# A gated attention and ReGLU backward pass: one matrix product and some transposes moved to other places

## The chip, the cores and the metric

The kernel runs on one core of a Trainium2 chip. The metric is device time in microseconds (us), the time of one execution on the chip. Times come from repeated runs; the profile comes from one execution of its own, whose time stands beside its span below.

## The reference

The reference computes a forward pass and its gradients with respect to seven inputs. Shapes: S = 2048 tokens, D = 512, F = 1376, 32 heads of 16, all bfloat16.

```python
qkv = (x @ wqkv).reshape(B, S, 3, H, Dh)...          # A: attention, window of 256 keys
p = softmax(where(mask, q k^T * Dh**-0.5, -1e9))
a = (p v) @ wo
gate = x @ W_gate; gate = gate * (gate > 0)          # B: ReGLU
h = gate * (x @ W_up)
b = h @ W_down
g = sigmoid((x * gate_w).sum(-1))
out = g * a + (1 - g) * b
# returned: out and the gradients of x, wqkv, wo, W_gate, W_up, W_down, gate_w for grad_out
```

## The kernel before, in words

There are three stages, and TensorE (PE) has one queue of instructions through all of them, in the order in which the program writes them. Most of it is written under a manual schedule, so the order on each engine is that of the Python code.

**FFN stage (0 to 251 us).** 44 steps: 11 chunks of F (128 columns each) by 4 groups of 512 tokens. A step computes gate, up and dh (`gate`, `up`, `dh`, L365 to L387), and some steps later the weight gradients of its chunk (`weights`, L402). The product h of a step is a tile hT with F on partitions and 512 tokens along the row. `turn_h` transposes it by DMA for the gradient of W_down, and `keep` (L398, called at L474) stores it to the DRAM tensor hT_d from ScalarE's DMA queue, as it does dgT and duT. The gradient of W_down of the last chunk is copied to the constant tile gw_b (L425), which later holds gate_w for the last stage. The activations db_r and db_T have tiles of their own in this stage.

**Attention stage (251 to 719 us).** Four head groups c of eight heads. In the profiled execution their first score matmuls start at 251.2, 354.1, 469.7 and 585.1 us. A group has 16 query tiles j of 128 tokens, and a query tile has up to six units: key block j ("d", diagonal), j - 1 ("m", middle) and j - 2 ("f", far), each in two halves of four heads. That makes 90 units a group, 360 in all. A unit is

- a score matmul ST of 512 columns (`front`, L681), its exponential on ScalarE (L691) and, for d and f, a mask on GpSimd (L693, L696), which gives Pu;
- a matmul dPT of 512 columns (`front_dp`, L705) one unit later, and the product Pd = Pu * dPT on VectorE (L710) two units later;
- 16 narrow matmuls of row sums (`rowsum`, L719 and L721) four units later, the value LAG;
- the transposes of Pu and Pd by 128 x 128 blocks (`flip`, L730). Where `u.dma` is set (L669), they are made by a DMA transpose on SP's queue, three units behind the front. Otherwise TensorE makes eight transposes (L748) into a PSUM tile pt, which ScalarE or VectorE copies out. Before, d units and m units of the first three groups go by DMA in pairs of halves (128 x 2048 elements), and all f units go by TensorE;
- later, 16 narrow matmuls CD per transposed unit (`cd_piece`, L532), which read the transposed tiles. The pieces wait in a list with the unit from which each may be issued: for the youngest query tile five units behind its last row sum.

PSUM tiles of tag TR (two banks) serve pt, the projections pp and the gradients wps in turn.

Between the units the planner (the `while` loop from L894) puts fillers: the six parts of the next projection (`project_parts`, L123: Q, dO, their DMA transpose, K, V, and the transposes of K and V), and pieces of the weight gradient of the group before (`grad_parts`, L623). A credit decides when: each unit adds SLOT - 0.63 us (L942), minus 0.44 if the unit that is LAG behind is transposed by TensorE; each filler takes its cost; a due time forces a projection that would come too late. Projected K and V lie in three buffers in rotation (one in pool pjA, two in pool pj). The table `plan` (L616) says behind which projection the weights of the last stage are loaded; those of W_down (`loads`, L599) and wo come last, in the fourth group.

**Last stage (719 to 910 us).** Eight groups of two query tiles. `load_group` (L817) loads, one group ahead, h (hT_g), dgT, duT, grad_out rows (go), attention outputs (o_g) and, by one DMA transpose from dqkvo_d, the tile T. hT, T and go of a group share one slot of pool st (tag rows_st, two buffers, also used by the rows of the head groups), the slots of the others come from pool g6. Per tile of 128 tokens TensorE runs dwo (4 matmuls of 512 columns, L1014), bps = h x W_down (11, L1033), aps (4, L1037), dxps from dgT and duT (22, L1060), four narrow dgw and dxps from T (12, L1064). This stage is ordered by the framework, not by hand.

Of the kernel before, what the change touches and what calls it, by code (L numbers as in the profile page):

```python
# [22 lines left out]
def kernel(  # L23
# [20 lines left out]
    nc = tc.nc  # L44
# [37 lines left out]
    hT_d = dram.tile([F, S], BF, name="hT_d")  # L82
# [29 lines left out]
    if True:  # L112
# [84 lines left out]

    with ExitStack() as p1, tc.manual_schedule():
# [3 lines left out]
        db_r = ap1.tile([P, NT, D], BF, name="db_r")  # L202
        db_T = ap1.tile([P, DC, S], BF, name="db_T")
# [198 lines left out]
        def weights(k):  # L402
# [25 lines left out]
            evac(dst[:], acc["d"][:], "act")  # L428

            def store():  # L430
# [4 lines left out]
                nc.sync.dma_start(out_6[k.fsl, :], dst[:])  # L435
# [6 lines left out]

        DA0 = 2 * NTG
# [4 lines left out]
        for n in range(N1 + 8):  # L448
# [24 lines left out]
            if at(3):  # L473
                keep(at(3), (hT_d, at(3).hT[:]))  # L474
# [30 lines left out]
            if n in (N1 + 2, N1 + 3, N1 + 4):  # L505
                second.pop(0)()
            z = n - DA0 - NT - 2
# [6 lines left out]
    if True:  # L514
        st = p3.enter_context(tc.tile_pool(name="attst", bufs=2))
# [70 lines left out]
        def load_rows(name, src, k, dst):  # L586
            W6[(name, k)] = dst
            skip = max(0, (k + 1) * P - src.shape[0])
            if skip:
                nc.gpsimd.memset(dst[0:skip, :], 0.0)  # L590
            nc.sync.dma_start(dst[skip:P, :], src[k * P:(k + 1) * P - skip, :])

# [6 lines left out]
        def loads(name, src, k0, tag):  # L599
            def one(k):  # L600
                if (tag, "t") not in W6:
                    W6[(tag, "t")] = slot(tag)
                load_rows(name, src, k, W6[(tag, "t")][:, k - k0, :])
            return [lambda k=k: one(k) for k in range(k0, min(k0 + 4, FC))]

        def load_wo():
            t = pjA.tile([P, 2, TGW], BF, tag="zT", name="wo_z")
            for k in range(2):
                load_rows("wo", A_wo, k, t[:, k, :])
            for k in range(2, DC):  # L610
                load_rows("wo", A_wo, k, pjA.tile([P, TGW], BF, tag="T", bufs=2, name="wo_t")[:])

        def load_gw():
            nc.sync.dma_start(gw_b[:], gate_w.partition_broadcast(P))

        plan = {2: [load_gw], 5: turns("wqkv", A_wqkv, 0, 4, "p0"), 7: turns("wqkv", A_wqkv, 4, 8, "p1"),  # L616
# [4 lines left out]
                15: loads("Wd", B_W_down, 0, "x3") + [lambda: clear("Wu")] + loads("Wd", B_W_down, 4, "d3") + loads("Wd", B_W_down, 8, "p3") + [load_wo]}  # L621
# [31 lines left out]

        class Unit:
# [3 lines left out]
        for c in range(DC):  # L658
            for j in range(NT):
                order = [(k, h) for k, h in ((j - 1, 0), (j - 1, 1), (j - 2, 0), (j, 0), (j, 1), (j - 2, 1)) if k >= 0]  # L660
                for kb, half in order:
# [7 lines left out]
                    u.dma = u.pair or (u.role == "m" and half == 0 and (c < DC - 1 or j < 10))  # L669
# [5 lines left out]
        def front(u):  # L675
# [6 lines left out]
            if not u.own:  # L682
                if u.half == 0:
                    kind = "m" if u.c == DC - 1 and u.j == 12 else u.role
                    tag = f"PP{kind}"
                    pairs[(u.c, u.j, u.kb)] = wk.tile([P, 2, 2, HH, P], BF, tag=tag, bufs=3, name=tag)
# [20 lines left out]
        def gradp(u):  # L707
            if u.own:
                u.Pd = wk.tile([P, HH, P], BF, tag="Pd", bufs=2, name="Pd")
# [102 lines left out]
        def early_f(i):  # L812
            flat = wq.tile([P, 2, TPG, NP, P], BF, tag=f"z{i}", name=f"f{i}")[:].rearrange("p w k h q -> p (w k h q)")
            S2[f"f{i}"] = flat[:, 0:FC * GT * P].rearrange("p (c s) -> p c s", c=FC)
            load_f(S2[f"f{i}"], (hT_d, dgT_d)[i], slice(0, GT * P))

        def load_group(g):  # L817
            gsl = slice(g * GT * P, (g + 1) * GT * P)
            if g == 0:
# [315 lines left out]
```

## Time and profile before

| What | Value |
|---|---|
| Time, median of 3 runs | 911.95 us (910.37 to 912.51) |
| Time of the profiled execution | 911.74 us |
| Its span, first to last instruction | 910.0 us |
| TensorE (PE) busy, instructions | 897.0 us (99%), 10711 |
| Weight loads (PEld) busy | 568.2 us (62%) |
| VectorE (DVE) busy | 510.3 us (56%) |
| ScalarE (ACT) busy | 443.2 us (49%) |
| GpSimd (POOL) busy | 494.2 us (54%) |
| Granted TensorE clock, whole span | 1.000 |
| DMA, whole span | 169.06 MB, mean 186 GB/s |

PE is TensorE's matmuls, PEld its weight loads, SP the engine whose queue issues most DMAs, ACTq and POOLq the DMA queues of ScalarE and GpSimd. L681 is line 681 of the kernel. A matmul is recorded from its issue to its modelled end, so that neighbours overlap. The DMA share is the mean busy share of 16 DMA engines; it can exceed 1, since several packets of one engine can be under way. The chain of waits follows the work that ended last back to what released it.

### The profile page before, as it was taken

To read this page: it belongs to the slowest core of one execution; us is meant where nothing else is said; L and a number is where in the kernel's file an instruction comes from. 1 tells how busy PE (TensorE), PEld (TensorE's weight loads), DVE (VectorE), ACT (ScalarE), POOL (GpSimd) and SP (SyncE) were. 2 spreads that over 40 slices of the span, in tenths; PEclk is the share of its full clock that TensorE was granted. 3 is DMA by queue.
4 is the path that set the end of the run, shared out by engine and by line. 5 is a ranking of instruction groups with operands and counts; after the bars stand their busy time and mean duration, and the time that the engine had idled before them with its cause. 6 is when DMAs were issued, how large, how long until landed. Compare 5 with 4: busy or idle time off the path is not lost. (4 is left out here: it accounts for less than half of the span.)

```text
span 910.0 us, 26129 instructions
## 1 busy us (share of the span) xinstructions
PE 897.0 (99%) x10711; PEld 568.2 (62%) x10711; DVE 510.3 (56%) x952; ACT 443.2 (49%) x778; POOL 494.2 (54%) x937
## 2 busy tenths in 40 slices
PE   8999999999989999999999999999999999999998
PEld 5565665655657777667776677766778644444445
DVE  3433434434368777668886788876787222233323
ACT  5422222222278777667776677766788211100001
POOL 3654445545267777767777678775677312222221
PEclk9999999999999999999999999999999999999999
DMA  9998889999799999999999999999999999777731
GB/s 299 196 188 195 189 188 209 213 218 212 179 160 159 177 187 182 190 171 167 180 186 173 187 166 182 185 176 187 168 190 178 232 261 237 181 187 179 185 87 46
DMA packets 505575, 169.06 MB, mean 186 GB/s; under 512 B 433456, under 2 KB 504336, under 8 KB 505456
## 3 DMA queue, kind: packets, MB, share of 16 engines
q1 hardware_dynamic: 484816, 145.51, 86.6%
q10 hardware_dynamic: 19008, 17.31, 6.6%
q0 software_dynamic: 1632, 4.59, 1.4%
q8 instruction: 83, 1.36, 0.6%
q14 instruction: 36, 0.29, 0.1%
HBM read 32.28 MB, written 36.24 MB: 75 GB/s over the span
## 5 line engine op out<-in xcount | busy, mean ns | idle before, releaser
L705 PE MATMUL dPT<-z,V 128*128 128x512 bf16 x360 | 135.9, 378 | 2.8 <-DVE PPm L710 0.9
L681 PE MATMUL ST<-z,K 128*128 128x512 bf16 x360 | 135.8, 378 | 2.1 <-ACT PPd L691 0.5
L693 POOL TENSOR_SCALAR_AFFINE_SELECT PPd<-PPd 128x512 bf16<-128x512 bf16 x126 | 80.1, 638 | 79.9 <-ACT PPd L691 79.3
L377 POOL TENSOR_TENSOR hT<-rg,upm 128x512 bf16<-128x512 bf16 x44 | 51.1, 1161 | 115.2 <-DVE upm L375 94.5
L412 PE MATMUL wps<-dgu_r,x_r 128*128 128x256 bf16 (+1 forms) x704 | 103.9, 270 | 0.3 <-DVE wst L74 0.3
L696 POOL TENSOR_SCALAR_AFFINE_SELECT Pu<-Pu 128x512 bf16<-128x512 bf16 x112 | 71.8, 641 | 38.9 <-ACT Pu L691 35.9
L710 DVE TENSOR_TENSOR PPd<-PPd,dPT 128x512 bf16<-128x512 bf16 x126 | 82.2, 672 | 11.1 <-PE dPT L705 5.3
L710 DVE TENSOR_TENSOR Pd<-Pu,dPT 128x512 bf16<-128x512 bf16 x112 | 76.1, 680 | 21.9 <-PE dPT L705 17.6
L691 ACT ACTIVATE PPm<-ST 128x512 bf16<-128x512 f32 x122 | 73.0, 600 | 31.2 <-PE ST L681 30.9
L412 PEld LDWEIGHTS <-x_r 128*128 128x128 bf16 x704 | 68.4, 98 | 31.2 <-issue 0.5
L710 DVE TENSOR_TENSOR PPm<-PPm,dPT 128x512 bf16<-128x512 bf16 x122 | 81.9, 680 | 9.2 <-PE dPT L705 7.7
L691 ACT ACTIVATE PPd<-ST 128x512 bf16<-128x512 f32 x126 | 76.0, 607 | 18.1 <-PE ST L681 15.9
L1040 ACT COPY a_sb<-aps 128x512 f32<-128x512 f32 x16 | 9.4, 586 | 151.4 <-issue 137.6
L691 ACT ACTIVATE Pu<-ST 128x512 bf16<-128x512 f32 x112 | 67.3, 601 | 28.4 <-PE ST L681 28.4
L375 DVE SCALAR_TENSOR_TENSOR upm<-rg,ups 128x512 bf16<-128x512 bf16 x44 | 30.1, 685 | 78.8 <-PE ups L363 41.4
L369 ACT ACTIVATE rg<-gps 128x512 bf16<-128x512 f32 x44 | 26.3, 599 | 88.6 <-PE gps L363 39.1
L414 PE MATMUL dps<-db_r,h_r 128*128 128x512 bf16 x176 | 66.7, 379 | 0.0
L72 ACT COPY p<-pt 128x1024 bf16<-128x1024 bf16 x61 | 62.2, 1020 | 3.7
L387 POOL TENSOR_TENSOR dgu<-dh_sb,rg 128x512 bf16<-128x512 bf16 x44 | 57.8, 1313 | 5.3 <-ACT dh_sb L383 5.3
L1046 POOL DMA_DIRECT2D out_dram<-o_sb x16 | 8.7, 542 | 89.6 <-DVE o_sb L1044 83.1
L637 PE MATMUL wps<-rows_st,x_r 128*128 128x384 bf16 x256 | 50.3, 325 | 0.0
L386 DVE TENSOR_TENSOR dgu<-dh_sb,upm 128x512 bf16<-128x512 bf16 x44 | 33.8, 769 | 29.0 <-ACT dh_sb L383 26.4
(193 smaller groups left out, 2382.1 us busy)
## 6 DMA issues: line engine op xcount, KB each, us to landing
dqkvo_d<-rows_st SPq DMA_DIRECT2D x15, 512.0 KB, 4.0
hT_d<-hT ACTq DMA_DIRECT2D x44, 128.0 KB, 2.5
dgT_d<-dgu ACTq DMA_DIRECT2D x44, 128.0 KB, 3.0
duT_d<-dgu ACTq DMA_DIRECT2D x44, 128.0 KB, 3.0
duT_g<-duT_d SPq DMA_DIRECT2D x8, 640.0 KB, 5.4
gt<-hT_d SPq DMA_DIRECT2D x7, 640.0 KB, 5.9
dgT_g<-dgT_d SPq DMA_DIRECT2D x7, 640.0 KB, 5.2
out_dram<-wst SPq DMA_DIRECT2D x20, 128.0 KB, 2.8
```

Source lines behind the costliest of these rows:

```text
L72: nc.scalar.copy(out, in_)
L377: nc.gpsimd.tensor_tensor(out=k.hT[:], in0=k.rg[:], in1=k.upm[:], op=ALU.mult)
L387: nc.gpsimd.tensor_tensor(out=k.duT, in0=dh_sb[:], in1=k.rg[:], op=ALU.mult)
L412: nc.tensor.matmul(acc["w"][:, c, 0:2 * nw], lhsT=x_r[:, t, c * P:(c + 1) * P], rhs=k.dgu_r[:, :, i, s0:P], start=(go_ and c % 2 == 0), st ...
L414: nc.tensor.matmul(acc["d"][:], lhsT=k.h_r[:, i, :], rhs=db_r[:, t, :], start=go_, stop=no_)
L637: nc.tensor.matmul(wps[:], lhsT=x_r[:, t, part * P:(part + 1) * P], rhs=sts[c][:, t, 0:3, :], start=first and t == t0, stop=last and t == ...
L681: nc.tensor.matmul(ST[:], lhsT=KTt[:, ksl], rhs=z[:, 0, :, jl, :], start=True, stop=True)
L691: nc.scalar.activation(u.Pu[:], ST[:], ACT.Exp)
L693: nc.gpsimd.affine_select(out=u.Pu[:], in_=u.Pu[:], compare_op=ALU.is_ge, fill=0.0, base=0, pattern=[[0, HH], [1, P]], channel_multiplier=-1)
L696: nc.gpsimd.affine_select(out=u.Pu[:], in_=u.Pu[:], compare_op=ALU.is_ge, fill=0.0, base=-1, pattern=[[0, HH], [-1, P]], channel_multiplier=1)
L705: nc.tensor.matmul(u.dPT[:], lhsT=VTt[:, ksl], rhs=z[:, 1, :, jl, :], start=True, stop=True)
L710: nc.vector.tensor_tensor(out=u.Pd[:], in0=u.Pu[:], in1=u.dPT[:], op=ALU.mult)
```

## The change

1. The product b = h x W_down (bps, 176 matmuls) leaves the last stage. It is made in the first head group as a new kind of filler, 16 tiles in pieces of 4, 4 and 3 matmuls (`b_parts`). To that end h is stored as h_d, by token tile, and read back two tiles ahead; W_down is loaded at the end of the FFN stage into a slot of pool st, which moves ahead of the FFN stage (db_r and db_T now take its two slots first), and its last rows into gw_b. A finished product is copied by ScalarE, stored to b_d in float32, and loaded by the last stage (b_g). Loads and stores of this are issued by ScalarE.
2. In the first group a rule of its own places fillers, by two phases: one for projection parts, one for pieces of the product.
3. 35 far units are turned by DMA: in the first group half 0 of each tile and half 1 of the odd ones, in the second and third half 0 of the odd ones. They have single transposes of 128 x 1024. Pu and Pd of a far unit share a tile PF for that, with four buffers; d and m units share six buffers PP where each had three.
4. The credit of the second and third group grows by 1.35 - 0.63 a unit; the first and fourth keep SLOT = 1.5.
5. K and V have two buffers in rotation where there were three, and the parts K, V and their transposes are held back until a unit `gate`.
6. gate_w is loaded behind projection 5 and no longer 2; the loads of W_down in the fourth group fall away; in the last stage dgT takes h's place in the slot with T, and the first group's duT is loaded early.

The diff, cut to its core:

```diff
-    hT_d = dram.tile([F, S], BF, name="hT_d")
+    h_d = dram.tile([NT, P, FC, P], BF, name="h_d")
+    b_d = dram.tile([S, D], F32, name="b_d")
...
-            pj = lambda: pjA if (c * NTG + tg) % 3 == 0 else pjs["b"]
+            pj = lambda: pjA if (c * NTG + tg) % 2 == 0 else pjs["b"]
...
+    st = ctx.enter_context(tc.tile_pool(name="attst", bufs=2))
...
-        db_r = ap1.tile([P, NT, D], BF, name="db_r")
-        db_T = ap1.tile([P, DC, S], BF, name="db_T")
+        db_r = st.tile([P, NT, D], BF, tag="rows_st", name="db_r")
+        db_T = st.tile([P, DC, S], BF, tag="rows_st", name="db_T")
...
-                dst = gw_b
+                dst = pjA.tile([P, 2, TGW], BF, tag="zT", name="dst_end")[:, 0, :]
...
+        def load_h(t):
+            ffb[t] = ffb["t"][:, (FC - 1) * D + (t % 2) * FC * P:][:, 0:FC * P].rearrange("p (c q) -> p c q", c=FC)
+            nc.scalar.dma_start(ffb[t], h_d[t])
+
+        def open_b():
+            ffb["t"] = st.tile([P, (FC - 1) * D + 2 * FC * P], BF, tag="rows_st", name="ffb")
+            ffb["w"] = ffb["t"][:, 0:(FC - 1) * D].rearrange("p (c n) -> p c n", c=FC - 1)
+            h2 = (FC - 1) // 2
+            for a, b in ((0, h2), (h2, FC - 1)):
+                nc.scalar.dma_start(ffb["w"][:, a:b, :], B_W_down[a * P:b * P, :].rearrange("(c p) d -> p c d", p=P))
+            for t in range(2):
+                load_h(t)
...
-                keep(at(3), (hT_d, at(3).hT[:]))
+                k3 = at(3)
+                nc.scalar.dma_start(h_d[k3.tg * TPG:(k3.tg + 1) * TPG, :, k3.fc, :].rearrange("t p q -> p t q"),
+                                    k3.hT[:].rearrange("p (t q) -> p t q", t=TPG))
...
+            if n == N1 - 4:
+                load_rows(B_W_down, FC - 1, gw_b)
+            if n == N1 + 3:
+                open_b()
...
-        pjs["b"] = p3b.enter_context(tc.tile_pool(name="pj", bufs=2))
+        pjs["b"] = p3b.enter_context(tc.tile_pool(name="pj", bufs=1))
...
+            def piece(t, a, b):
+                if a == 0:
+                    hold[t] = psr.tile([P, D], F32, tag="TR", bufs=2, name="bps")
+                for k in range(a, b):
+                    nc.tensor.matmul(hold[t][:], lhsT=ffb[t][:, k, :], rhs=ffb["w"][:, k, :] if k < FC - 1 else gw_b[:],
+                                     start=(k == 0), stop=(k == FC - 1))
+                if b < FC:
+                    return None
+                bst = wk.tile([P, D], F32, tag="bst", bufs=1, name="bst")
+                nc.scalar.copy(bst[:], hold[t][:])
+
+                def after():
+                    nc.scalar.dma_start(b_d[t * P:(t + 1) * P, :], bst[:])
+                    if t + 2 < NT:
+                        load_h(t + 2)
+                        return t + 2
+                return after
...
-                    u.dma = u.pair or (u.role == "m" and half == 0 and (c < DC - 1 or j < 10))
+                    u.dma = u.pair or (u.own and (c == 0 and (half == 0 or j % 2) or c < DC - 1 and half == 0 and j % 2)) or (u.role == "m" and half == 0 and (c < DC - 1 or j < 10))
...
-                u.Pu = wk.tile([P, HH, P], BF, tag="Pu", bufs=2, name="Pu")
+                u.PP = wk.tile([P, 2, HH, P], BF, tag="PF", bufs=4, name="PF")
+                u.Pu, u.Pd = u.PP[:, 0, :, :], u.PP[:, 1, :, :]
...
+            if u.dma and u.own:
+                p2 = wk.tile([P, 2, HH, P], BF, tag="P2f", bufs=4, name="p2f")
+                nc.sync.dma_start_transpose(out=p2[:].rearrange("p a h q -> p (a h) q"),
+                                            in_=u.PP[:].rearrange("p a h q -> p (a h q)"))
+                P2[(u.c, u.j, u.kb, u.half)] = p2[:]
+                return
...
+            nc.sync.dma_start(b_g[:], b_d[gsl, :].rearrange("(t p) d -> p t d", p=P))
...
+                            gate = n + (12 if u.j else 5)
...
-                credit += SLOT - 0.63 - (0.44 if LAG <= n < NU + LAG and not units[n - LAG].dma else 0.0)
+                credit += (SLOT if (n - LAG) // C1 in (0, DC - 1) else 1.35) - 0.63 - (0.44 if LAG <= n < NU + LAG and not units[n - LAG].dma else 0.0)
...
+                elif u.c == 0:
+                    phase["p"] = min(1.2, phase["p"] + 0.21)
+                    phase["b"] = min(3.0, phase["b"] + len(bq) / max(1, C1 - 5 - n))
+                    turn = len(prq) == 4
+                    if prq and (len(prq) > 3 or n >= gate) and n > fed + 1 and (turn or phase["p"] >= 1 or due - n <= len(prq) + 1):
+                        phase["p"] -= not turn
+                        project()
+                    elif bq and phase["b"] >= 1 and n >= ready_b.get(bq[0][0], n + 1):
+                        phase["b"] -= 1
+                        b_piece()
...
-                    bps = ps6r.tile([P, D], F32, tag="bps", bufs=1)
-                    for fc in range(FC):
-                        nc.tensor.matmul(bps[:], lhsT=hT_g[:, fc, lsl], rhs=W6[("Wd", fc)],
-                                         start=(fc == 0), stop=(fc == FC - 1))
```

More of the change, by code (lines that the diff above doesn't have):

```diff
@@ L597, in turns @@
             return [lambda s=s: turn_w(name, src, s, tag, s[0] - k0) for s in sets]
[L599 to L604, printed above, removed]
         def load_wo():
             t = pjA.tile([P, 2, TGW], BF, tag="zT", name="wo_z")
[L608 to L611, printed above, removed]
+            for k in range(DC):
+                W6[("wo", k)] = t[:, k, :] if k < 2 else pjA.tile([P, TGW], BF, tag="T", bufs=2, name="wo_t")[:]
+                load_rows(A_wo, k, W6[("wo", k)])
         def load_gw():
             nc.sync.dma_start(gw_b[:], gate_w.partition_broadcast(P))
-        plan = {2: [load_gw], 5: turns("wqkv", A_wqkv, 0, 4, "p0"), 7: turns("wqkv", A_wqkv, 4, 8, "p1"),
+        plan = {5: [load_gw] + turns("wqkv", A_wqkv, 0, 4, "p0"), 7: turns("wqkv", A_wqkv, 4, 8, "p1"),
                 11: turns("wqkv", A_wqkv, 8, 12, "p2"),
@@ L1047 @@
                     amb = t6.tile([P, D], F32, tag="amb")
-                    nc.vector.tensor_tensor(out=amb[:], in0=a_sb[:], in1=bps[:], op=ALU.subtract)
+                    nc.vector.tensor_tensor(out=amb[:], in0=a_sb[:], in1=b_g[:, tl, :], op=ALU.subtract)
                     nc.gpsimd.tensor_tensor(out=amb[:], in0=amb[:], in1=go_g[:, tl, :], op=ALU.mult)
```

91 lines of the change are left out of this document (51 added, 40 removed).

## The prediction

> **What bounds the kernel.** I read first how much of each stage TensorE is busy, by stage: 0 to 251 us is the FFN, then four head groups, then the last stage. After the stretch come its length and the busy time (with the count) of PE, weight loads, VectorE, ScalarE and GpSimd, the granted clock, the DMA share and GB/s.
>
> ```profile
> 0.00:251.20 251.20, 247.81 (x1645) 151.11 (x1646) 102.49 (x160) 80.67 (x139) 116.84 (x104) 1.00 0.94 207
> 251.20:354.10 102.90, 99.69 (x1757) 69.54 (x1756) 81.14 (x155) 81.14 (x144) 77.36 (x179) 1.00 1.03 173
> 354.10:469.70 115.60, 115.17 (x2011) 81.06 (x2008) 88.15 (x168) 83.95 (x150) 85.36 (x197) 1.00 1.06 177
> 469.70:585.10 115.40, 115.04 (x2009) 81.00 (x2006) 88.44 (x169) 83.38 (x149) 85.38 (x197) 1.00 1.08 180
> 585.10:719.00 133.90, 131.63 (x2351) 96.30 (x2348) 92.71 (x169) 92.31 (x162) 92.29 (x215) 1.00 1.07 186
> 719.00:910.00 191.00, 187.64 (x963) 89.16 (x961) 57.39 (x134) 21.72 (x39) 37.01 (x48) 1.00 0.71 174
> ```
>
> TensorE is busy nearly all the time in every stage. But a matmul's recorded time (378 ns for 512 columns) is longer than the step to the next one, so busy time alone proves little. The steps do. In the chain of waits of the last stage (start, length, what):
>
> ```profile
> 734.01 2.37 PE bps L1033 x11
> 736.38 0.86 PE aps L1037 x4
> 737.24 4.75 PE dxps L1060 x22
> 741.99 0.08 PE dgw_ps L1085 x4
> 742.07 2.61 PE dxps L1064 x12
> 744.68 0.86 PE dwo L1014 x4
> 745.54 2.38 PE bps L1033 x11
> ```
>
> A 512-column matmul takes 2.37/11 = 0.216 us, and one query tile 745.54 - 734.01 = 11.53 us, all of it matmuls back to back. In a head group, eight transposes of a far unit:
>
> ```profile
> 302.97 0.38 PE L748 MATMUL pt<-ident,Pu 128*128 128x128 bf16 x4
> 303.19 0.39 PE L748 MATMUL pt<-ident,Pd 128*128 128x128 bf16 x4
> 303.42 0.38 PE L705 MATMUL dPT<-z,V 128*128 128x512 bf16 x1
> ```
>
> Eight in 303.42 - 302.97 = 0.45 us, 55 ns each. Counting every matmul at its undisturbed step (216, 162, 109 and 55 ns for 512, 384, 256 and 128 columns, 25 ns for 16 to 50) gives 96.0 us of the first head group's 102.9, 113.2 of the second's 115.6, the same for the third, and 883 us of all 910. So the time is TensorE's own queue, and only 27 us are lost, 8 before the attention and about 7 in the first head group, where 4.5 us lie in its first 20 us. What is taken off TensorE counts in full; what is moved along it counts nothing.
>
> **The sum.** The profiled execution took 911.74 us (span 910.0), 0.21 us under the median of 911.95.
>
> 1. *The 35 far units*: 21 in the first group (half 0 of 14 tiles, half 1 of the 7 odd ones), 7 in each of the next two. 35 x 8 = 280 transposes x 55 ns = **-15.4 us** (9.2, 3.1, 3.1). Their 35 copies (1.02 us on ScalarE or 0.69 on VectorE) go too, off the path.
>
> 2. *h x Wdown*: 16 x 11 = 176 matmuls x 0.216 = 38.0 us leave the last stage (a tile falls from 11.53 to 9.16 us) and 38.0 us enter the first head group: **0**. What it adds on other engines there: 16 ScalarE copies at about 0.59 us (row of a_sb, same shape, 586 ns) and 36 DMA issues at some 0.4 us, 24 us; less some 14 us of dropped copies; ScalarE then has 91 us of work in 125. Two waits are new. The copy of a product waits for the store of the one before (one bst buffer), which lands in some 3 us, with 124.8/16 = 7.8 us a tile; behind it on ScalarE stand the exps that TensorE's dPT needs. And a product holds one of the two TR banks for its three pieces, so projections and transposes share the other and wait for its copy, 0.6 to 1.0 us, if they follow each other at once; in the order of the built program another unit lies between. Both at 0, at most 16 x 0.6 = 10 us. The pieces also fill TensorE's gaps while the group starts: 0 to -4.5 us.
>
> 3. *DMA of the first group*. TensorE's need there becomes 96.0 + 38.0 - 9.2 = 124.8 us. The queue carried 102.9 x 173 GB/s = 17.8 MB; added are 21 x 0.262 = 5.5 MB of transposes, 5.8 of h, 4.2 of the product, 1.3 of Wdown: 34.6 MB, 277 GB/s over 124.8 us. This is the doubtful term. The DMA view of the group (slices of 2.6 us):
>
> ```profile
> DMA  1499999995939999999999789999999993999998
> GB/s 42 116 187 208 213 106 263 213 101 122 184 69 201 178 177 188 209 125 249 117 275 196 118 168 209 137 192 213 102 251 107 323 191 80 199 177 114 248 179 169
> p2d<-PPd SPq DMA_TRANSPOSE x15, 4.9
> p2m<-PPm SPq DMA_TRANSPOSE x15, 6.0
> rows<-zT SPq DMA_TRANSPOSE x3, 3.0
> ```
>
> The share reads 9 at 69 GB/s and at 263 alike, so it is no measure of what is left. Slices of transposes alone reach 249 to 275. At those rates 21.5 MB of transposes take about 80 us and 13 MB of plain transfers, at the 299 GB/s of the page's first slice, 43: 123 us, just inside 124.8. And SP waited for its producers, not for room: in this group
>
> ```profile
> SPq L738 <- DVE PPd L710: 16.3, 12, 3.3
> SPq L738 <- PE dPT L705: 15.3, 5, 3.6
> SPq L738 <- PE CD L544: 11.3, 5, 2.8
> ```
>
> A far transpose has the shape of rows<-zT, 3.0 us to landing (4.6 at most). By the code it is issued 3 units behind its front, and its CD matmuls come 6 (half 1) to 9 units later: 8.3 us or more at 124.8/90 = 1.39 us. Ahead of it on SP stands at most one d pair, whose issue holds SP about 2.3 us (median; 4.3 at most). So it lands in time as a rule. I take the group's loss as unchanged, 7 us: what the early pieces fill (some 3 us), waits for late transposes give back: **0**, ends -4.5 and +26 (rival B).
>
> 4. *Second and third group*: 1.8 MB more on 20.5 each, 199 GB/s over 112 us. The loss was 2.4 us; I add 1 each: **+2**, ends 0 and +6.2 (rival C). The lower credit (1.35 for 1.5) and the wait of K and V for their now two buffers only move fillers between units.
>
> 5. *The last stage's loads*. T of tiles 2 and 3 (gt<-dqkvo_d) was issued at 736.5 and landed at 745.3, behind dgT and duT of both groups; its first reader came at 747.9. Its slot is free only once the last store of the head groups has landed, at 726.4, 5 us into the stage, so it doesn't move forward with the shorter tiles: the first reader comes three products of 2.37 us earlier, at 740.8, while 1.4 MB of h are replaced by 1.0 MB of products, about 1 us less queue: 744.3. It comes 3.5 us late; with the stage's first loads a little lighter I take **+3**, ends 0 and +5. Later groups load in some 11 us behind the end of the group two before, in 18.3 us: hidden. Loads of Wdown (11 x 128 KB) fall away.
>
> 6. *The store of h* in 256-byte pieces, 512 a step for 128 of 1 KB, 44 times. out_dram<-wst, in 256-byte pieces, landed in 2.8 us; out_dram<-dst, in 1 KB, in 2.8. TensorE lost nothing from 40 to 230 us: **0**. Queue q10 took 6.6% of 910 us for 132 stores, 20 us for those of h; twice that is 20 us more beside 251, of which I allow 5 to show: ends 0 and +5. The Trainium skill ("DMA: Bandwidth & Descriptors", Specifications) says that pieces under 512 B cost a read-modify-write, which speaks against this layout. The two rows just named show no such cost; were the time of these stores doubled by it, the sum would end at the +5.
>
> Sum: -15.4 + 0 + 0 + 2 + 3 + 0 = -10.4: 911.74 - 10.4 = 901.3, and with the 0.2 to the median **901.5 us**.
>
> **Rivals.**
>
> *B, slower: the DMA engines become the bound of the first group.* If the busiest 14.5 us of this group (199 GB/s over 318.5 to 333) is all that transposes can do, 21.5 MB take 108 us, and the rest 43: 151 us for 124.8, +26: 927; with half of that, 914. It decides where the group's DMA falls under 34.6/(124.8 + 7 + 10.4) = 243 GB/s. For it: share 1.03 already. Against it: 249 to 275 GB/s in single slices. The Trainium skill ("DMA: Bandwidth & Descriptors", Latency and other measured facts) gives DMA transposes 261 GB/s in one case and more where the data is contiguous; the slices agree, and an estimate by that page is 82 + 43 = 125 us, the forecast's case.
>
> *C: the second and third group don't follow TensorE.* VectorE has 88 us of 115.6; with the far transposes landing late, the 6.2 us taken off there are lost in waits: 907.5. Against it: 24% of VectorE is free.
>
> *D: loads of the last stage come late in each group*, not once: SP's chain of go, dgT and T (0.4 + 1.1 + 6 issue, 8.7 to landing) starts at the end of the group two before, and o_g and duT stand in its way. 1.5 us in each of 7 groups is +10: 911, no change. Against it: 11 us of 18.3.
>
> *E: better*: the gaps at the start are filled and no transpose is late: -15.4 - 4.5: 892, or 895 with term 5.
>
> **Chances and range.** Forecast (896 to 906) 0.62; C 0.10; D 0.05; B 0.13; E 0.10. Leaving out E's lower and B's upper part gives 895.5 to 914. This kernel's measurement tells 0.2%, 1.8 us, from no change. Faster: forecast, E and most of C, 0.80; same: D and a little of C and B, 0.06; slower: B and the rest, 0.14.
>
> **What the new profile would show.** bps pieces in the first group and none later; that group 128 to 135 us long, and 9.16 us a tile in the last stage; 752 transposes under pt for 1032. If TensorE's CD matmuls wait for p2f, or the group is over 140 us at some 240 GB/s, B holds; if aps of the third tile waits some 3 us for gt, term 5. Groups two and three at 115 us again would be C. The forecast is wrong above all if the DMA of the first group stays under 243 GB/s.

## The result, and the profile after

The changed kernel takes **937.08 us** (median of 4 runs, 931.72 to 939.64) beside 911.58 us for the kernel before on the same chip: ratio 1.0273, 95% interval 1.0224 to 1.0321. It is slower; the prediction was 901.5 us with a range to 914. The profiled execution took 931.72 us (span 929.8), 20.0 us more than the profiled execution of before.

Busy time by stage of the changed kernel, with the columns of the first table of the prediction; the stages now begin at 249.2, 401.8, 520.1, 637.0 and 762.2 us:

```profile
0.00:249.20 249.20, 244.20 (x1613) 149.86 (x1645) 100.14 (x160) 80.31 (x138) 117.05 (x105) 1.00 0.96 214
249.20:401.80 152.60, 130.89 (x1754) 79.59 (x1779) 78.22 (x148) 79.27 (x148) 77.67 (x179) 0.97 1.11 212
401.80:520.10 118.30, 111.71 (x1935) 77.59 (x1945) 85.38 (x164) 77.90 (x145) 83.86 (x196) 1.00 1.14 189
520.10:637.00 116.90, 111.86 (x1933) 77.69 (x1946) 86.49 (x165) 78.86 (x145) 85.66 (x197) 1.00 1.17 190
637.00:762.20 125.20, 119.23 (x2098) 86.89 (x2105) 89.04 (x164) 87.90 (x154) 85.96 (x199) 0.97 1.06 182
762.20:930.00 167.80, 162.47 (x1008) 81.94 (x1019) 60.23 (x139) 25.05 (x46) 47.90 (x63) 1.00 0.78 199
```

The same view of the kernel before, cut at the last front of its fourth group (the prediction's table cut later):

```profile
585.10:704.70 119.60, 117.92 (x2116) 86.13 (x2113) 90.02 (x165) 88.68 (x155) 85.32 (x197) 1.00 1.08 182
704.70:910.00 205.30, 201.36 (x1198) 99.33 (x1195) 60.07 (x139) 25.34 (x46) 43.98 (x67) 1.00 0.73 177
```

After less before, stage by stage: -2.0, **+49.7**, +2.7, +1.5, +5.6, **-37.5**; the sum is +20.0. The last stage gives about what was forecast (38.0 out, 3 for late loads). The first head group, forecast 29 us longer (38.0 in, 9.2 out), is 49.7 longer, and no other group becomes shorter.

The last stage is TensorE's own, and a tile takes 853.97 - 844.81 = 9.16 us, as forecast (chain of waits of the changed kernel; start, length, what):

```profile
844.81 0.86 PE aps L1100 x4
...
853.97 0.86 PE aps L1100 x4
```

In the first head group TensorE waits for other things than before. Its waits there (line, who is waited for: us in all, times, longest):

```profile
PE CD L569 <- DMA p2f<-PF: 13.9, 6, 3.9
PE bps L676 <- ACT dst_end L72: 4.8, 1, 4.8
PE bps L676 <- DMA ffb<-h_d: 0.8, 2, 0.4
```

The first line is the sign that the prediction had named for rival B: the CD matmuls wait for the far transposes. The DMA view of the same stretch (queues with packets, MB and share; transposes with the median us from issue to landing):

```profile
q1 hardware_dynamic: 85871, 22.36, 89.6%
q10 hardware_dynamic: 4518, 9.71, 20.9%
...
p2f<-PF SPq DMA_TRANSPOSE x19, 4.1
p2d<-PPd SPq DMA_TRANSPOSE x15, 6.6
p2m<-PPm SPq DMA_TRANSPOSE x15, 6.2
```

All queues together, SP's (q1) and ScalarE's (q10) above all, carry 32 MB at 212 GB/s, under the 243 that the prediction had set as the line between its forecast and rival B. p2d lands in 6.6 us where before showed 4.9, and the far transposes come on top.

Two smaller losses are new. At the start of the group (order of time; start, length, engine, what, and in brackets the idle time before it and what ended it):

```profile
253.79 0.58 ACT L72 CAST dst_end<-dps 128x512 bf16<-128x512 f32 x1 [4.07 <-DMA rows<-zT]
...
254.42 1.86 PE L676 MATMUL bps<-ffb 128*128 128x512 bf16 x4 [4.83 <-ACT dst_end L72]
```

ScalarE's copy of W_down's last gradient chunk now goes into the slot of zT, and has to wait until the transposition that reads zT has landed. Behind it on ScalarE wait the exps, and the first bps needs the PSUM bank that it frees. And in the fourth group:

```profile
731.63 0.51 POOL L612 MEMSET d<- 32x512 bf16 x1 [7.26 <-DMA d<-in_B_W_up_dram]
...
733.51 0.58 PE L720 MATMUL ST<-z,K 128*128 128x512 bf16 x1 [4.50 <-DVE PF L746]
```

The clear of W_up's last rows on GpSimd now stands directly behind the DMA transposes whose target it clears; the loads of W_down that stood between are gone. GpSimd waits 7.3 us, the masks of the next units stand behind it, VectorE's gradp behind them, and TensorE is empty for 4.5 us.

Last, the granted clock, which before held 1.00 throughout (stage view, two stretches cut out):

```profile
253.90:257.30 3.40, 2.88 (x7) 1.01 (x7) 0.06 (x1) 1.52 (x3) 0.64 (x1) 0.50 0.11 39
...
731.70:738.50 6.80, 4.99 (x71) 3.33 (x71) 4.29 (x8) 2.80 (x4) 5.88 (x14) 0.50 1.02 225
```

Behind the long gaps of TensorE the clock is 0.50: 3.4 us at 253.9, 356.3 and 397.2, 6.8 at 731.7, 17.0 us in all (0.991 over the span; 0.980 to 0.989 in the other three runs, which are the longer ones).

### The profile page after: what moved, and what is told of

The parts are those of the page before. It is cut to its first block, busy times and chain, and to the rows that moved or that the text cites. A ratio compares the mean times of both kernels' runs of the same rounds, so it can differ in the third digit from the quotient of the medians.

```text
span 929.8 us, 25618 instructions
## 1 busy us (share of the span) xinstructions
PE 880.4 (95%) x10323; PEld 553.6 (60%) x10431; DVE 499.5 (54%) x939; ACT 429.3 (46%) x772; POOL 498.1 (54%) x937
## 5 line engine op out<-in xcount | busy, mean ns | idle before, releaser
L720 PE MATMUL ST<-z,K 128*128 128x512 bf16 x360 | 137.7, 382 | 6.7 <-DVE PF L746 4.7
L734 POOL TENSOR_SCALAR_AFFINE_SELECT PF<-PF 128x512 bf16<-128x512 bf16 x112 | 71.6, 639 | 59.9 <-ACT PF L729 59.4
L746 DVE TENSOR_TENSOR PF<-PF,dPT 128x512 bf16<-128x512 bf16 x112 | 76.4, 682 | 40.9 <-PE dPT L743 11.2
L746 DVE TENSOR_TENSOR PPd<-PPd,dPT 128x512 bf16<-128x512 bf16 x128 | 84.3, 673 | 24.0 <-PE dPT L743 15.2
L729 ACT ACTIVATE PF<-ST 128x512 bf16<-128x512 f32 x112 | 67.3, 601 | 44.0 <-PE ST L720 28.4
L423 PE MATMUL dps<-db_r,h_r 128*128 128x512 bf16 x159 | 60.3, 379 | 0.0
L790 PE MATMUL pt<-ident,PF 128*128 128x128 bf16 x616 | 48.0, 222 | 0.0
L1134 POOL DMA_DIRECT2D out_dram<-dx_sb x15 | 8.1, 541 | 73.9 <-DVE dx_sb L1132 69.0
L676 PE MATMUL bps<-ffb 128*128 128x512 bf16 x140 | 40.2, 393 | 6.8 <-ACT dst_end L72 4.8
```

The source lines that it names most:

```text
L423: nc.tensor.matmul(acc["d"][:], lhsT=k.h_r[:, i, :], rhs=db_r[:, t, :], start=go_, stop=no_)
L720: nc.tensor.matmul(ST[:], lhsT=KTt[:, ksl], rhs=z[:, 0, :, jl, :], start=True, stop=True)
L729: nc.scalar.activation(u.Pu[:], ST[:], ACT.Exp)
L734: nc.gpsimd.affine_select(out=u.Pu[:], in_=u.Pu[:], compare_op=ALU.is_ge, fill=0.0, base=-1, pattern=[[0, HH], [-1, P]], channel_multiplier=1)
L746: nc.vector.tensor_tensor(out=u.Pd[:], in0=u.Pu[:], in1=u.dPT[:], op=ALU.mult)
L790: nc.tensor.transpose(pt[:, a, hh, :], src[:, hh, :], ident[:])
```

## The experiments

Theory: four losses. The DMA engines can't turn the far units of the first group in time; the copy at the group's start waits; the clear blocks GpSimd; and half clock follows the gaps. Rivals: one of the small ones, or the moved product itself, makes the group late. Each ratio is to the kernel before in runs on the same chip, with its 95% interval.

**1. The clear, later.**

```diff
-                15: [lambda: clear("Wu"), load_wo]}
+                15: 4 * [lambda: None] + [lambda: clear("Wu"), load_wo]}
```

> Only the order of the fourth head group's late list is changed: four empty entries go ahead of the GpSimd clear of W_up's last rows, so that it is issued 16 steps later, as in the kernel before. Theory (clear blocks GpSimd): the 4.64 us gap of TensorE at 733.5 us goes, and the 6.8 us at half clock behind it, so 4.6 + 3.4 = 8 us less than the changed kernel, 924 in a profile like its 931.7; fourth group 117 to 120 us instead of 125.2. Rival (the group is late by its DMA anyway, the gap only comes first): another wait takes its place and the time stays within 2 us.

927.48 us, 1.0197 (1.0152 to 1.0242), some 7 us less than the changed kernel's 1.0273. In the profiled run the fourth group takes 118.7 us at clock 1.00, for 125.2. The theory holds. (The profiled execution, 934.88 us, is the longest of the four: its first group took 159.0 us, with 15.2 us of waits for p2f. That loss differs from run to run.)

**2. The last gradient chunk in a place of its own.**

```diff
-                dst = pjA.tile([P, 2, TGW], BF, tag="zT", name="dst_end")[:, 0, :]
+                dst = ffb["s0"][:, NT - 1, :, :].rearrange("p a n -> p (a n)")
...
+            ffb["s0"] = st.tile([P, NT, 4, P], BF, tag="rows_st", name="rows_st")
...
```

> Only the home of the last gradient chunk of W_down at the end of the feed-forward stage is changed: it goes to the still unwritten last rows of the first group's row store instead of the zT slot, so ScalarE's copy no longer waits for the transposition that reads zT. Theory (that wait holds ScalarE and the PSUM bank): the 5.00 us gap of TensorE at 254.4 us goes and the 3.4 us at half clock with it, 5 to 6.7 us less; 925 to 927 in a profile like the changed kernel's 931.7, first head group 146 to 148 us instead of 152.6. Rival (the first group is as long as its DMA engines need): the group still ends at about 401, what is saved at its start is waited for later at the products that read p2f, and the time stays within 2 us.

931.72 us, 1.0224 (1.0177 to 1.0270), by the ratios 4.5 us less, though the intervals meet. The wait for dst_end is gone (1.0 us for ffb is left) and the group takes 148.3 us, but it still waits 10.0 us for p2f, and once 3.1 us for a late exp: part of the gain is given back.

**3. The first group's far units back on TensorE.**

```diff
-                    u.dma = u.pair or (u.own and (c == 0 and (half == 0 or j % 2) or c < DC - 1 and half == 0 and j % 2)) or (u.role == "m" and half == 0 and (c < DC - 1 or j < 10))
+                    u.dma = u.pair or (u.own and 0 < c < DC - 1 and half == 0 and j % 2) or (u.role == "m" and half == 0 and (c < DC - 1 or j < 10))
```

> Only the 21 far units of the first head group are turned on TensorE again; the 14 of the second and third stay with DMA, and the moved product h x Wdown stays. Theory (the DMA engines are full in the first group and p2f comes late): the 14.8 us of waits for p2f and 1.7 us of half clock behind them go, 21 x 8 x 55 ns = 9.2 us of transposes come back: 7 us less, first head group about 145, the rest of what it lost (start 5 + half clock 1.7) stays; other tiles (p2d, rows) may still be late. Rival (DMA volume of h, b and W_down is what fills the engines, and the diagonal and middle tiles will be late in turn): first group stays above 150, time within 2 us or longer by up to 9 us.

922.25 us, 1.0118 (1.0100 to 1.0136): 15 us less than the changed kernel, with 9.2 us more for TensorE to do. No wait for p2f is left in the group (144.5 us); the largest is again dst_end, 4.2. From profile to profile the gain is 7.7 us, as expected. The medians show twice that: the changed kernel's profiled execution was the shortest of its four (5.4 us under their median), this one's the longest (1.8 over).

**4. h loaded for two tiles only.** b of tiles 2 to 15 is then the product of h of tiles 0 and 1.

```diff
-            nc.scalar.dma_start(ffb[t], h_d[t])
+            if t < 2:
+                nc.scalar.dma_start(ffb[t], h_d[t])
```

> The loads of h for token tiles 2 to 15 are left out: the product h x Wdown uses the h of tiles 0 and 1 again (b is then not the reference's); all instructions on TensorE stay. 14 x 0.36 = 5.0 MB of the first group's 32.35 MB fall away, 16%. Theory (the DMA engines are full): the group's transfers need 15% less, at least 10 of the 14.8 us of waits for p2f go and the group is 138 to 142 us; total 8 to 13 us less than the changed kernel. Rival (what makes p2f late is the rate at which one queue turns 128x128 blocks, or the order on the SP queue, not the engines' volume): p2f waits stay at 10 us or more and the group above 148.

920.36 us, 1.0103 (1.0067 to 1.0139). The group takes 137.7 us, 14.9 less, for 32.35 - 26.88 = 5.5 MB less, and waits 3.2 us for p2f instead of 13.9. No instruction of TensorE or SP was taken out, only 14 issues on ScalarE, and TensorE's waits for ScalarE (4.2 us, all dst_end, for 5.1) hardly change: the traffic on ScalarE's queue is what makes SP's transposes late.

**5. The far units alone, in the kernel before.**

```diff
-                    u.dma = u.pair or (u.role == "m" and half == 0 and (c < DC - 1 or j < 10))
+                    u.dma = u.pair or (u.own and (c == 0 and (half == 0 or j % 2) or c < DC - 1 and half == 0 and j % 2)) or (u.role == "m" and half == 0 and (c < DC - 1 or j < 10))
```

with the PF, P2f, two-buffer and `gate` lines of the change (K and V have two buffers here too).

> The kernel before with the 35 far units alone turned by DMA; h x Wdown stays in the last stage, the loads of W_down stay, the credit stays 1.5. (To make room, the projections use two sets of K/V instead of three, gated as in the changed kernel.) Theory (the DMA engines bound it): the first head group of before moved 62,578 packets of 256 bytes in 102.9 us; with 21 x 1,024 more it is 84,000, and at the 832 a microsecond that its dense stretches show that is 101 us, so the group is 101 to 104 us instead of 102.9 although TensorE needs 9.2 us less; second and third groups 116 to 118 as in the changed kernel instead of 115.5: total between 910 and 916. Rival (it is the moved product's transfers alone that fill the engines): first group 94 to 96, the others 113, total 895 to 900, the 15.4 us of the prediction.

932.29 us, 1.0235 (1.0216 to 1.0253). Both expectations miss, the first (910 to 916) in size only: this part, which was to bring -15.4 us, costs 21. Stage view of its first group:

```profile
250.80:373.30 122.50, 100.60 (x1592) 64.86 (x1604) 77.30 (x148) 71.55 (x132) 78.31 (x180) 0.92 1.11 185
```

122.5 us for the 102.9 of before, with 9.2 us less to do for TensorE: no plain traffic was added, and 81.5 thousand packets of 256 bytes went through at 81.5/122.5 = 665 a microsecond, 170 GB/s. SP's queue in order of time (start, length of the issue):

```profile
341.13 1.25 SPq L735 DMA_TRANSPOSE p2f<-PF  x1
342.47 2.02 SPq L743 DMA_TRANSPOSE p2d<-PPd  x1
344.59 1.80 SPq L735 DMA_TRANSPOSE p2f<-PF  x1
```

One issue ends 0.1 us before the next begins: the issues fill nearly the whole group, and the queue is hardly ever empty. Yet the transposes don't flow evenly. The DMA view of 12 us of it (40 slices of 0.3 us):

```profile
DMA  9999995000699999998999999999990000999998
GB/s 218 216 170 153 290 155 3 0 9 9 134 289 290 288 290 273 237 204 138 210 225 207 217 216 218 213 179 194 270 115 0 4 9 10 257 337 379 375 239 222
```

Twice, at 339.8 and 347, the DMA engines nearly stand still for more than 1 us. In the packet records of the group there are 16 such stops, in which 256-byte packets that else take 18 ns take 0.5 to 1.9 us; together they last 20.8 us. Each comes less than 1 us behind a packet of 8 or 16 KB on the two queues that the view calls instruction (q8 and q14), which have 17 such packets in the group. So the 170 GB/s are not a smooth rate: about a sixth of the time is stops. What makes them isn't shown, and no run is without those packets.

**6 to 8. The moved product with its start and clear mended** (edits 1 and 2), and three numbers of far units: 14 (edit 3: none in the first group), none at all, and 21 (7 in each of three groups, half 0 of the odd tiles; the edit from 14 to 21 is shown). The two sets of K/V, the placing of fillers and the credit of the change stay in all three.

```diff
-                    u.dma = u.pair or (u.own and 0 < c < DC - 1 and half == 0 and j % 2) or (u.role == "m" and half == 0 and (c < DC - 1 or j < 10))
+                    u.dma = u.pair or (u.own and c < DC - 1 and half == 0 and j % 2) or (u.role == "m" and half == 0 and (c < DC - 1 or j < 10))
```

> The changed kernel with three mends together: the clear 16 steps later, the last gradient chunk of W_down in the row store, the 21 far units of the first group back on TensorE (14 far units of groups two and three stay with DMA). Theory (three separate losses, each shown alone): they add up, 922.3 of the third mend alone less 6.5 (clear) less 5 to 6 (start) = 910 to 911, the time of before; first group 137 to 139. Rival (they hide each other): 914 or more.

> As the run with three mends, but the 14 far units of the second and third group go back to TensorE too, so that only h x Wdown is moved. Theory (in groups two and three the far units gave nothing: the waits for p2f and the small waits took more than the 7 x 8 x 55 ns = 3.1 us a group): groups two and three 115 to 117 instead of 116 to 118, total 1 to 4 us below the run with 14 far units, 907 to 910. Rival (they pay their 6.2 us, and the waits there come from the credit or from two sets of K/V): total 3 to 6 us above that run.

> As the run with three mends, but 7 far units of the first group (one in three of the 21) are turned by DMA as in the second and third. Theory (the engines are full in the first group from the first 256-byte packet on): the 3.1 us of transposes saved come back as waits for p2f: within 2 us of the run with 14 far units, or slower. Rival (there is room for some of them once the start is mended): 3 us less than that run.

14 far units: 912.17 us, 1.0013 (1.0001 to 1.0025). The mends add up nearly as expected (910 to 911; first group 138.7 us). None: 913.77 us, 1.0032 (1.0016 to 1.0048). 21: **907.22 us, 0.9952 (0.9935 to 0.9968)**, half a per cent faster than the kernel before. The stage view of the first group, without far units there (second of the three kernels):

```profile
249.30:387.80 138.50, 133.62 (x1903) 85.73 (x1931) 81.99 (x155) 91.32 (x160) 78.50 (x179) 1.00 0.96 199
```

and with 7 (third):

```profile
251.60:386.60 135.00, 130.99 (x1858) 83.05 (x1884) 81.83 (x153) 88.01 (x156) 78.63 (x179) 1.00 1.05 216
```

So the moved product without far units costs little: 138.5 us for 102.9 + 38.0 = 140.9, and 169.0 for 205.3 in the last stage (in a profiled execution 2.4 us under the median). The expectation for none was wrong in sign: taking the 14 back costs 1.6 us in the medians, with intervals that overlap, so the second and third group's far units bring between nothing and 3.5 us of their 6.2. The 7 in the first group pay their 3.1 us in full: the group falls from 138.7 to 135.0 us, the median by 5.0, and there the rival was right.

**9. The far units alone, issued on ScalarE's queue** (edit against experiment 5).

```diff
-                nc.sync.dma_start_transpose(out=p2[:].rearrange("p a h q -> p (a h) q"),
+                nc.scalar.dma_start_transpose(out=p2[:].rearrange("p a h q -> p (a h) q"),
```

> The kernel before with the 35 far units alone turned by DMA, as in the run that took 932 us, but these 35 transpositions are issued on ScalarE's queue, the 30 + 30 + 3 of the other kinds stay on SP. In that run SP issued one transposition behind the other without a pause in the first group (sum of its issues 118 of 122.5 us, 81.5 thousand packets of 256 bytes, 665 a microsecond). Theory (the DMA engines turn no more than about 665 packets a microsecond together): the group stays at 119 to 124 us, each SP issue lasts about as long, total 928 to 935. Rival (SP's own issuing, 1.2 us and more for 1,024 packets, is the limit): SP needs 30 us less, the group falls below 110, total below 918, as far as ScalarE (busy 0.63 of the group, plus 21 issues) lets it.

1083.37 us, 1.1889 (1.1870 to 1.1909). Both expectations miss, and it can't decide the question. ScalarE in order of time, with the idle time before:

```profile
338.69 1.25 ACTq L735 DMA_TRANSPOSE p2f<-PF  x1
339.98 0.37 ACT L547 CAST rows_st<-CD 128x256 bf16<-128x256 f32 x1 [5.91 <-issue]
```

The program lets a transposition on ScalarE's queue wait until those of SP's queue have landed: SP issued p2d at 334.34, p2d needs 4.2 to 6.3 us there from issue to landing, and ScalarE's p2f follows at 338.69. The copies and exps stand behind it, so that ScalarE is idle for 5.9 us. The Trainium skill ("DMA: Bandwidth & Descriptors", Latency and other measured facts) says that two DMA transposes in flight on different queues corrupt each other and must be serialized, which is what these waits do; what happens without them wasn't tried.

**10. The far units alone, with traffic that nobody reads** (edit against experiment 5; what is on SP's queue is unchanged).

```diff
+    scr = dram.tile([NT, 88, S], BF, name="scr")
...
+                    if u.first and u.c == 0 and u.j > 0:
+                        ev.setdefault(n + 1, []).append(("dma", lambda j=u.j: nc.scalar.dma_start(scr[j], dgT_d[0:88, :])))
```

> The kernel before with the 35 far units turned by DMA (first group 122.5 us, 932 us in all), with 15 plain copies of 360 KB, DRAM to DRAM, added on ScalarE's queue, one at each query tile of the first group: 5.4 MB of traffic that nobody reads, and no instruction of TensorE, VectorE, GpSimd or SP changed. Theory (the DMA engines are the limit): leaving out 5.0 MB of h loads made that group 14.9 us shorter in the changed kernel, so 5.4 MB make this one 10 to 18 us longer: 133 to 140 us, total 942 to 950, and p2f waits of 25 us or more. Rival (SP's issuing is the limit): the group stays within 3 us of 122.5.

943.29 us, 1.0352 (1.0332 to 1.0373). The first group in the stage view, and its longest wait of TensorE:

```profile
251.50:387.00 135.50, 104.72 (x1603) 66.46 (x1602) 77.33 (x148) 71.85 (x132) 78.35 (x179) 0.86 1.11 207
PE CD L543 <- DMA p2f<-PF: 23.7, 7, 5.8
```

13.0 us more for 28.00 - 22.63 = 5.4 MB, 2.4 us per MB (2.7 in experiment 4). The waits for p2f grow from 15.4 to 23.7 us, a little under the 25 expected; most of the rest is TensorE's own work at a lower clock (0.86 for 0.92), so the price of a MB has some half clock in it. SP's 60 issues, the same as in experiment 5, hold it 128 us for 116, and the waits for ScalarE's exps stay under 2 us. So what is limited is the DMA engines, or what lies behind them for all queues, and not SP's issuing alone. The Trainium skill ("DMA: Bandwidth & Descriptors", Issuing engines are not separate DMA queues) says that transfers of all issuing engines run on the same 16 DMA engines; this run agrees.

**11. 7 far units in each of three groups of the kernel before.** (Experiment 5 with only `c < DC - 1 and half == 0 and j % 2`.)

> The kernel before with 7 far units turned by DMA in each of the first three groups, 21 in all (two sets of K/V; h x Wdown stays in the last stage). Theory (rate): the first group has 62.6 + 7.2 = 69.8 thousand packets of 256 bytes; at the 665 a microsecond of the run with 21 there, that is 105 us, 2 us more than before, although TensorE needs 3.1 us less; groups two and three 115 to 118; total 911 to 916, no gain, whereas the same 21 units gained 6 us beside the moved product, which stretches the first group to 135. Rival (7 units fit in anywhere): first group 100, groups two and three 113 to 115, total 903 to 907.

916.19 us, 1.0045 (1.0031 to 1.0059), at the upper end of the theory. First group 103.0 us, no shorter; the second 120.3 for 115.6, with 4.0 us of waits for p2f. The 21 units that beside the moved product lead to 0.9952 cost 4 us here. But this kernel also has the credit at 1.5. With the moved product and the same credit (the second kernel of the next experiments) the ratio is 1.0005, so that only the step from 1.0045 to 1.0005, some 4 us, can be put down to the product and the mends that go with it. Credit 1.35 without the product was not run.

**12 to 14. From the 907 us kernel: 14 far units in the first group; the credit at 1.5. And the changed kernel with all far units and only the two mends.**

```diff
-                    u.dma = u.pair or (u.own and c < DC - 1 and half == 0 and j % 2) or (u.role == "m" and half == 0 and (c < DC - 1 or j < 10))
+                    u.dma = u.pair or (u.own and c < DC - 1 and half == 0 and (c == 0 or j % 2)) or (u.role == "m" and half == 0 and (c < DC - 1 or j < 10))
...
-                credit += (SLOT if (n - LAG) // C1 in (0, DC - 1) else 1.35) - 0.63 - (0.44 if LAG <= n < NU + LAG and not units[n - LAG].dma else 0.0)
+                credit += SLOT - 0.63 - (0.44 if LAG <= n < NU + LAG and not units[n - LAG].dma else 0.0)
```

> The same fastest run with 14 far units of the first group turned by DMA instead of 7. With 7 that group took 134.9 us and 69.8 thousand packets of 256 bytes (517 a microsecond) beside 11 MB of other transfers; with 21 and the start not mended 152.6 us and 82.0 thousand (537 a microsecond). Theory (a rate of about 535 a microsecond beside these transfers is the limit): 7 x 1,024 packets more are 77.0 thousand, 144 us: group 141 to 146, total 913 to 918, slower than with 7. Rival (late p2f in the changed kernel came from waits of single transpositions, not from the rate): 3.1 us less, group 132, total 904.

> The fastest run so far (moved product, three mends, 7 far units in each of three groups, 907.2 us) with the credit of the second and third group back at 1.5 instead of 1.35. Theory (the credit only moves fillers within a group): within 1.5 us of 907.2, groups two and three 113 to 118. Rival (the lower credit is what keeps fillers from running ahead of the transpositions): second or third group longer by 2 us or more.

> The changed kernel with all its 35 far units, mended in two places only: the clear 16 steps later and the last gradient chunk of W_down in the row store. Theory (the losses add up): 937 less 7 less 5 = 923 to 927, first group 147 to 150 with 10 to 16 us of waits for p2f; what is left against the run with 7 far units there, 907, is the price of the other 14. Rival: the mends need the far units back on TensorE to count, total above 930.

With 14: 915.17 us, 1.0047 (1.0023 to 1.0071), 8 us slower than with 7. Its first group is 138.8 us, a little under the 141 to 146 expected, and the second 3.6 us longer, into which late transposes run over. In the first group TensorE waits 3.4 us for late exps and 2.8 for ffb, which the edit doesn't touch, but not for p2f.

With credit 1.5: 910.81 us, 1.0005 (0.9990 to 1.0020), slower than with 1.35; both expectations miss. In its profile (914.0 us, 3.2 over its median) the second and third group are only 1.5 and 0.4 us longer. 3.0 lie in the first group, where a wait for ffb (2.5 us) and half clock came at the start, and 2.4 in the last stage, places that the edit doesn't touch. How much of the 3.6 us is the credit's stays open.

With all 21 and the two mends: 923.83 us, 1.0156 (1.0123 to 1.0190), as expected; its first group, 151.3 us with 13.4 us of waits for p2f, is a little over the 147 to 150 expected.

## Why the prediction was wrong

**Term 3 is the step that failed**: "At those rates 21.5 MB of transposes take about 80 us". The volume was not the mistake (32.35 MB moved, for 34.6 counted); the rate was. It was that of the best slices of 2.6 us, 249 to 275 GB/s, and the 275 was not of transposes alone: in that slice of before, 1228 of 1612 packets are under 512 bytes, 0.31 of 0.71 MB at most. Turned without a pause, as experiment 5 does it, transposes reach 170 GB/s: 20.9 MB in 122.5 us, with its stops in it. Beside that, each MB of other traffic took 2.4 to 2.7 us (experiments 10 and 4). Without its own 1.8 MB of other traffic (4 us), experiment 5 needs some 118 us for the transposes; the changed kernel's 11.4 MB x 2.6 = 30 us on top make 148. Measured are 152.6, of which 4.8 are the wait at the start (148.3 without it, in experiment 2). The 148 is an estimate, and not an independent one, since the 2.7 comes from the changed kernel itself. The 261 GB/s of the Trainium skill ("DMA: Bandwidth & Descriptors", Latency and other measured facts), which the slices had agreed with, was not reached over any group.

The prediction also read SP's waits for its producers as room on the queue. The issue times say more: in the first group of before they hold SP 82 of 102.9 us (p2d 15 x 2.70, p2m 15 x 2.25, the rest 8; the 2.3 us that the prediction gives for a d pair is the median of the whole run, in this group it is 3.0). The 19 far ones that fall into the group, at 1.6 us (as experiment 5 shows them), make 113. That is over the 94 to which TensorE's need would have shrunk the group in experiment 5, but under the 125 of the changed kernel. There the other traffic decides: it stretched SP's issues to 140 of 152.6 us.

**Term 1** (-15.4) counted TensorE's instructions rightly and the time wrongly: alone, the 35 units cost 21 us, 19.6 of them in the first group, which is at once bound by their transposes. **Rival B** had the mechanism. Its price of the group (151 us; measured 152.6) is in part luck: it took 108 us for the transposes and 43 for the rest, where the runs give some 118 and 30, and the start's wait of 4.8 was in none of its terms. Its chance of 0.13 was too low: the evidence against it was single slices.

**Term 2** was right: without far units and with the start and the clear mended, moving 38 us costs 1.0032 (1.0016 to 1.0048), the two sets of K/V and the new credit included, and neither the bst buffer nor the TR banks shows a wait over 1 us. What it left out is one line of the diff: dst_end in the zT slot, 4.8 us of wait at the group's start.

**Term 4** (-6.2 + 2 for two groups) came out +4.2. Rival C, the far units' gain lost in waits for late transposes, fits what these groups show, and it was somewhat short. They turn 77.5 thousand packets in 117 to 118 us, 660 a microsecond, as many as the first group of experiment 5 (665). That they lie at the same limit is concluded from this rate; no run tests it there.

**Term 5**: the wait of aps for gt was 0.8 us in the profile (3 forecast; 1.5 to 2.6 in the other runs of the moved product). But "Loads of Wdown fall away" was priced at nothing, and they had kept the clear away from the transposes before it: some 7 us by experiment 1. What then stands next on GpSimd's queue was not followed.

**Term 6** was right: the FFN stage is 2.0 us shorter, not longer (between 249.3 and 251.6 us in the other runs of the moved product, for 251.2).

**What no term had** is the clock. A gap of 4.0 us or more, and some shorter ones, is paid for again: TensorE runs at half clock for 3.4 us or a multiple, which costs up to half of that.

In sum, by medians: 937.1; 923.8 with the start and the clear mended; 915.2, 907.2 and 912.2 with 14, 7 and none of the first group's far units left on DMA; 913.8 with none anywhere. The best of these gains 4 us where 10 were forecast. The moved product stretches the first group by 32 to 36 us, in which 7 more transposes fit; its own 10 MB on the engines, at 2.4 to 2.7 us each, take most of that room again. Without the product the same 21 units cost 4 us; at an equal credit the difference is some 4 us, and the rest of the way to 907.2 isn't explained.

## What to carry to other kernels

Before moving work from TensorE to DMA transposes, add up how long the issues hold their queue over the whole stage, the moved ones included, and compare it with the stage's new length; the rate of a short slice doesn't answer that, and neither do waits of the queue for its producers. Transfers on another queue come out of the same engines and must be added in: here 113 us of issues seemed to fit into 125, and 9.7 MB on ScalarE's queue, at 2.4 to 2.7 us each, would bring them to 136 to 139 by estimate (140 measured). When a list of late steps loses entries, look at what now stands directly behind a DMA on every engine's queue.

## What the runs showed of the hardware

Half clock comes behind gaps that are not long. Behind every TensorE gap of 4.0 us or more in these profiles the granted clock was 0.50 for 3.4 us or a multiple (6.8, and 13.7 in experiment 9); but also behind one of 1.75 us (at 347.7 in experiment 4), and not behind ones of 2.5 (at 487.6 in the changed kernel) and 3.0 us (at 339.2 in experiment 1). In the changed kernel the stretches begin 102.4, 40.9 and 334.5 us apart, whole multiples of 3.41. The Trainium skill ("TensorE: Matmul & The Clock Gate", What's actually happening) says that the clock falls to half after an idle window of about 3.4 us, and that the windows run freely. The lengths and the fixed raster agree; a gap well under a whole window was enough here, which that rule doesn't say.

The rate of DMA transposes falls with the time over which it is taken. By the starts of the 256-byte packets in the first group of before, the best 2 us have 289 GB/s, the best 10 us 197 and the best 40 us 168; in experiment 5, where the queue is full, it is 289, 207 and 183, and 170 over the whole group.
